# A fused attention and two-layer mixture kernel: gathering tokens into two buffers two groups ahead, an earlier table, and outputs block by block

## The chip, the cores and the metric

The kernel runs on one core of one Trainium2 chip. It uses five engines: TensorE (PE in the rows; PEld is its weight load), VectorE (DVE), ScalarE (ACT), GpSimd (POOL) and SyncE (SP), which only issues DMAs here. The metric is device time in microseconds of one execution; the median of the timed runs counts. One execution was taken with the hardware profiler.

## The reference

Three layers, all in float32:

```python
p_packed = sm_attn(p, k, v)              # 8 batches, 8 heads, 576 tokens, 32 packed rows, head size 64
out = sm_attn(q, p_packed, p_packed)
x = out.transpose(0, 2, 1, 3).reshape(4608, 512)
h = x @ w_in                             # 512 -> 2048
x = (h / (1 + exp(-h))) @ w_out          # 2048 -> 512
e = argmax(x @ w_gate, axis=1)           # one of 8 experts per token
for each expert:                         # 512 -> 1024 -> 512
    y = maximum(x[mask] @ w1[e], 0) @ w2[e]
    out[mask] = gate_w * sigmoid(x @ w_output_gate)[e] * y
```

`gate_w` is the softmax weight of the chosen expert. How many tokens an expert gets depends on the data.

## The kernel before

The first 800 us compute attention and the first mixture layer, batch by batch. Each block of 128 finished tokens is written to the DRAM table `xr` (a row is the 512 values and the gate weight), and its token numbers are scattered to the DRAM list `perm`, sorted by expert (`place`, L809). Matrix products are split: each float32 operand is a high and a low part, and three products are added. The expert weights were split earlier and lie in DRAM as `ws1` and `ws2`.

The change lies in the expert stage. Its unit is a **group**: 576 tokens of one expert, gathered through `perm`. Eight groups are laid out in the program (`NSTATIC`), more follow behind a branch that this data doesn't take. Group 0 is the largest expert's first 576 tokens, picked early. The others come from a table (`table`, `spread`) that is worked out once the last tokens are placed: expert and offset for each group, in the SBUF tile `tab`.

A group has 8 hidden slices of 128. For each slice n there is an **up projection** (`up`, L1002: 24 matmuls into the one PSUM tile `pu`), a handover (ScalarE takes the rectified high part, VectorE the low part, L1007 and L1008, into a ring of three), and a **down projection** (`down`, L1024 and L1027: 14 matmuls into five PSUM blocks of tokens). TensorE's order is up(n+1), gap, down(n), gap. The next up needs the handover of the one before, since `pu` has one buffer.

What else is to be done is hung into these **gaps** by number (`self.gaps`, 16 per group; group k owns gaps 16k to 16k+15). A step that is hung there is issued to its engines at that place of the program; each engine has its own queue and runs it in order.

- `fetch(g)`: SyncE reads expert and offset from `tab`, then orders the index table `xix` (from `perm`, L915 and L916) and the expert's gate row `og` (L934). GpSimd sets the unused indices (L914) and issues five indirect DMAs that gather the token rows to `xg` (L925).
- `trx(g, j)`: TensorE transposes block j of the gathered tokens (`px`, L966, one PSUM bank), ScalarE and VectorE copy and split it to `xt` (L971, L972); a gap later VectorE and ScalarE compute the output gate (`gate_dot`).
- `load_chunk`: SyncE orders a weight chunk of 2 MB for two slices (L950, L952) into a ring of five; it waits until the chunk that lay there has been used.
- `put_out(g, j)`, behind the last slice: ScalarE scales block j from PSUM to `y` (block 4 has two halves to add and goes over VectorE as well), and GpSimd scatters the rows to the output (L1046, an indirect DMA).

Gathered tokens, index tables and gate rows have one, three and one buffer. `plan` hangs the transposes of group k+1 into group k's gaps 5, 7, 9, 11 and 13 and the fetch of group k+2 into gap 15; in group 0 the transposes stand in gaps 12, 13, 14, 14 and 14. Behind the last group all engines load the number of groups from `tab` (L860) and branch.

Of the kernel before, what the change touches and what calls it, by code (L numbers as in the profile page):

```python
# [21 lines left out]
DM = 512  # L22
# [8 lines left out]
GB = 5  # L31
# [56 lines left out]
class Kernel:  # L88
# [762 lines left out]
    def experts(self):  # L851
        nc = self.nc
        g = self.group_l
        self.gaps = {0: [lambda: self.row_t(g, 4), self.load_chunk], 1: [lambda: self.row_logits(g, 4)], 2: [self.load_chunk],
                     3: [lambda: self.place(g)], 4: [self.table], 7: [self.spread, lambda: self.fetch(1)]}
        for i in (10, 13, 14, 15):
            self.gaps[i] = [self.load_chunk]
        self.plan(0, NSTATIC, 12, 1)
        self.groups(0, NSTATIC)
        t = nc.values_load(self.tab[0:1, 2, 0:1], min_val=0, max_val=NGRP)  # L860
        with self.tc.If(t > NSTATIC):
            self.more(NSTATIC, NSTATIC + 2)
            with self.tc.If(t > NSTATIC + 2):
                self.more(NSTATIC + 2, NGRP)

    def more(self, lo, hi):
        self.nload = 4 * lo
        self.fetch(lo)
        for _ in range(4):
            self.load_chunk()  # L870
        for j in range(GB):
            self.trx(lo, j)
        run(self.late)
        run(self.late)
        if lo + 1 < hi:
            self.fetch(lo + 1)
        self.plan(lo, hi)
        self.up(FG * lo)
        self.groups(lo, hi)

    def plan(self, lo, hi, first=5, every=2):
        for k in range(lo, hi - 1):
            at = [16 * k + (first + j * every if k == lo else 5 + 2 * j) for j in range(GB)]
            for j, n in enumerate(at):
                n = min(n, 16 * k + 14)
                self.gaps.setdefault(n, []).append(lambda k=k, j=j: self.trx(k + 1, j))
            if k + 2 < hi:
                self.gaps.setdefault(min(at[-1], 16 * k + 14) + 2, []).append(lambda k=k: self.fetch(k + 2))

# [9 lines left out]
    def groups(self, lo, hi):  # L899
        self.gap(2 * FG * lo)  # L900
        for n in range(FG * lo, FG * hi):
            if n + 1 < FG * hi:
                self.up(n + 1)
            self.gap(2 * n + 1)
            self.down(n)
            if n % 2 and n > 6 and self.nload < 4 * hi:
# [3 lines left out]
    def fetch_ix(self, g, off):  # L910
        nc = self.nc
        off = nc.values_load(off, engines=[ENG.SP], min_val=0, max_val=END)
        at = self.rt.tile([128, GB], I32, tag="xix", bufs=3, name="xix")
        nc.gpsimd.memset(at[64:128, 4:5], NTOK)  # L914
# [14 lines left out]
    def fetch(self, g):  # L929
        nc = self.nc  # L930
        self.expert(g)
        self.fetch_ix(g, self.tab[0:1, 0, g:g + 1])
        og = self.p2.tile([128, DM], F32, tag="og", name="og")
        nc.sync.dma_start(og, self.i["wog"][bass.ds(self.ex[g], 1), :].to_broadcast([128, DM]))  # L934
        x = self.rt.tile([128, GB, XW], F32, tag="xr", name="xg")
        self.x[g] = [x[:, j] for j in range(GB)], og
# [73 lines left out]

    def down(self, n):
        nc = self.nc
        g, ff = divmod(n, FG)
        w = self.chunk[n // 2][:, 2048:].rearrange("p (r k c) -> p r k c", r=2, k=2)[:, :, ff % 2, :]
        if ff % 2:
            self.chunk.pop(n // 2)
        hl = self.hl.pop(n)
        if ff == 0:
            self.acc = [(self.ps_acc if j < 4 else self.ps_a).tile([128, 512], F32, tag=f"acc{j}", name="py") for j in range(GB)]
        first, last = ff == 0, ff == FG - 1  # L1020
        for j in (4, 0, 1, 2, 3):
            if j == 4:
# [5 lines left out]
            if last:  # L1028
                self.put_out(g, j)
        if last:  # L1030
            self.at.pop(g)

# [52 lines left out]
```

## Time and profile before

| | us |
|---|---|
| median of 3 timed runs | 1304.09 (1303.91 to 1305.34) |
| profiled execution, its own time | 1306.18 |
| its span, first to last instruction | 1304.40 |
| TensorE matmul busy | 1213.3 |
| VectorE, ScalarE, GpSimd busy | 656.5, 472.6, 167.7 |

The expert stage begins at about 815 us. Busy times of TensorE are long where the clock is low, so idle time and the granted clock are read together. A row of the timeline may merge several instructions of a kind (x24); a bracket says how long the engine was idle before it and what its release is put down to. For TensorE the duration of a merged row reaches to the modelled end of its last matmul.

### The profile page before, as it was taken

How to read it: one execution, taken by the hardware profiler on the slowest of the kernel's cores; microseconds unless marked ns; L12 is line 12 of the kernel's file. 1: busy time of each engine (PE TensorE's matmuls, PEld its weight loads, DVE VectorE, ACT ScalarE, POOL GpSimd, SP SyncE). 2: the span in 40 equal slices, each digit the busy share in tenths (PEclk: the TensorE clock that was granted, in tenths of full speed). 3: DMA queues.
4: the chain of work that ended last, by engine and by line, in shares of the span. 5: the costliest groups of instructions: out<-in, count | busy, mean ns of one | idle time of the engine just before them, and what ended most of it. 6: DMA issues, size and time to landing. Idle time of an engine off the chain costs nothing. (4 is left out here: it accounts for less than half of the span.)

```text
span 1304.4 us, 22047 instructions
## 1 busy us (share of the span) xinstructions
PE 1213.3 (93%) x8758; PEld 1003.9 (77%) x8760; DVE 656.5 (50%) x1495; ACT 472.6 (36%) x978; POOL 167.7 (13%) x211
## 2 busy tenths in 40 slices
PE   7697998999998999999999999999989898998996
PEld 3575786877787787787777788898989898898995
DVE  6888658457657357658457545323313232232311
ACT  3333554454554354554454433112122121212221
POOL 0334101000101000101000401113020220302011
PEclk9898999999999999999999999999989999999998
DMA  8664468456767465867464711459454554637311
GB/s 304 214 182 168 166 231 267 169 206 229 269 217 253 164 233 200 260 230 252 172 217 161 213 48 34 124 209 322 175 206 158 214 203 178 215 133 273 132 37 39
DMA packets 118725, 250.26 MB, mean 192 GB/s; under 512 B 13363, under 2 KB 64374, under 8 KB 118358
## 3 DMA queue, kind: packets, MB, share of 16 engines
q1 hardware_dynamic: 111318, 228.66, 51.5%
q0 software_dynamic: 7296, 20.11, 4.2%
q8 instruction: 71, 1.16, 0.4%
q14 instruction: 40, 0.33, 0.1%
HBM read 160.17 MB, written 88.70 MB: 191 GB/s over the span
## 5 line engine op out<-in xcount | busy, mean ns | idle before, releaser
L741 PE MATMUL acc<-wo,ghi 128*128 128x512 f32 x1024 | 318.6, 392 | 0.0
L1002 PE MATMUL pu<-xt,w 128*128 128x256 f32 (+1 forms) x1536 | 224.6, 304 | 17.3 <-DVE xt L1008 17.3
L1002 PEld LDWEIGHTS pu<-xt,w 128*128 128x128 f32 x1536 | 218.0, 197 | 24.0 <-issue 19.4
L741 PEld LDWEIGHTS acc<-wo,ghi 128*128 128x128 f32 x1024 | 193.1, 189 | 38.3
L1008 DVE SCALAR_TENSOR_TENSOR xt<-pu,xt 128x512 fp32r<-128x512 f32 (+1 forms) x128 | 58.7, 458 | 325.3 <-ACT xt L1007 323.3
L741 PE MATMUL acc<-wo,glo 128*128 128x512 f32 x512 | 212.0, 414 | 0.0
L690 PE MATMUL ps_h<-a,m_hi 128*128 128x288 f32 x1024 | 211.2, 299 | 0.8 <-DVE a L656 0.8
L1027 PE MATMUL py<-w,xt 128*128 128x512 f32 x768 | 188.2, 393 | 0.2 <-issue 0.2
L690 PE MATMUL ps_h<-a,m_lo 128*128 128x288 f32 x512 | 161.4, 315 | 28.4 <-DVE g L700 19.6
L1007 ACT ACTIVATE xt<-pu 128x512 fp32r<-128x512 f32 (+1 forms) x128 | 52.5, 410 | 355.0 <-PE pu L1002 246.9
L1027 PEld LDWEIGHTS py<-w,xt 128*128 128x128 f32 x768 | 144.2, 188 | 34.3 <-issue 0.6
L690 PEld LDWEIGHTS ps_h<-a,m_hi 128*128 128x128 f32 x1024 | 167.3, 192 | 2.5 <-DVE a L656 1.0
L700 DVE SCALAR_TENSOR_TENSOR g<-g,ps_h 128x576 f32<-128x576 f32 x128 | 96.1, 750 | 133.2 <-ACT g L699 132.8
L699 ACT ACTIVATE g<-ps_h 128x576 f32<-128x576 f32 x128 | 83.3, 651 | 172.8 <-PE ps_h L690 160.2
L690 PEld LDWEIGHTS ps_h<-a,m_lo 128*128 128x128 f32 x512 | 97.8, 191 | 55.3 <-DVE g L700 28.9
L741 PEld LDWEIGHTS acc<-wo,glo 128*128 128x128 f32 x512 | 96.6, 189 | 45.6 <-issue 27.0
L809 POOL DMA_INDIRECT perm<-tok,dsti x36 | 39.0, 1083 | 653.9 <-DVE dsti L805 517.3
L710 DVE TENSOR_TENSOR glo<-g,ghi 128x512 fp32r<-128x512 f32 x128 | 91.5, 715 | 38.2 <-ACT ghi L705 33.7
L705 ACT CAST ghi<-g 128x512 fp32r<-128x512 f32 x128 | 79.4, 620 | 73.8 <-DVE g L700 72.3
L510 DVE TENSOR_TENSOR mid<-mid,shi 128x1024 fp32r<-128x1024 f32 x48 | 58.8, 1226 | 43.2 <-ACT shi L509 43.2
L925 POOL DMA_INDIRECT xg<-xr,xix x35 | 33.4, 955 | 239.6 <-DVE yl L1044 214.7
L561 PE MATMUL ps_m<-w_in,ppt 64*32 64x256 f32 x1008 | 44.8, 402 | 10.3 <-ACT e L577 6.1
(188 smaller groups left out, 1173.1 us busy)
## 6 DMA issues: line engine op xcount, KB each, us to landing
w<-ws SPq DMA_DIRECT2D x64, 1024.0 KB
ws<-shi SPq DMA_DIRECT2D x64, 512.0 KB
mid<-in_w SPq DMA_DIRECT2D x48, 512.0 KB
ws<-mid SPq DMA_DIRECT2D x48, 512.0 KB
att_v<-in_v SPq DMA_DIRECT2D x15, 640.0 KB
att_k<-in_k SPq DMA_DIRECT2D x15, 576.0 KB
xr<-xr SPq DMA_DIRECT2D x32, 256.5 KB
stg<-in_w_in SPq DMA_DIRECT2D x16, 512.0 KB
```

Source lines behind the costliest of these rows:

```text
L510: nc.vector.tensor_tensor(out=w.bitcast(F32R), in0=w, in1=hi.bitcast(F32), op=ALU.subtract)
L561: self.nc.tensor.matmul(ps[32 * c:32 * c + 32, r, :n], lhs(rows, c), rhs(rows, c), start=True, stop=True)
L690: nc.tensor.matmul(ps[:, hf, :288], lw[:, qd, fs], rx[:, qd, ts], start=(i == 0), stop=(i == 5))
L699: nc.scalar.activation(out=g2, in_=ps[:, :, :288], func=AF.Tanh, scale=0.5)
L700: nc.vector.scalar_tensor_tensor(out=g2, in0=g2, scalar=1.0, in1=ps[:, :, :288], op0=ALU.add, op1=ALU.mult)
L705: self.nc.scalar.copy(out=hi, in_=self.graw[:, :512])
L710: self.nc.vector.tensor_tensor(out=lo, in0=self.graw[:, :512], in1=self.ghi.bitcast(F32), op=ALU.subtract)
L741: self.nc.tensor.matmul(acc, l, r, start=(first and i == 0), stop=(last and i == 2))
L1002: nc.tensor.matmul(ps[:, hf, :m], w[:, k, r, fs], xt[:, l, k, ts], start=(i == 0), stop=(i == 11))
L1007: nc.scalar.activation(out=hi, in_=src, func=AF.Relu)
L1008: nc.vector.scalar_tensor_tensor(out=lo, in0=src, scalar=0.0, in1=hi.bitcast(F32), op0=ALU.max, op1=ALU.subtract)
L1027: nc.tensor.matmul(self.acc[j], hl[:, l + j * 128:l + j * 128 + 128], w[:, r], start=(first and i == 0), stop=(last and i == 2))
```

## The change

Gathered tokens have two buffers, one for odd and one for even groups, gate rows two and index tables four. The fetch of group k+2 stands in gap 3 of group k instead of gap 15; those of groups 1 and 2 in gaps 5 and 11 of group 0. In group 0 the last placement, the table and the spread stand in gaps 2, 3 and 5 (were 3, 4 and 7), a chunk load in 8 (was 10) and the five transposes in gaps 10 to 14. The number of groups is loaded six gaps before the end. In the last group the down projections of the last two slices are issued together, block by block, with each block's output behind it, in the order 0, 4, 1, 2, 3.

```diff
--- before.py
+++ after.py
@@ -851,17 +851,21 @@
     def experts(self):
         nc = self.nc
         g = self.group_l
-        self.gaps = {0: [lambda: self.row_t(g, 4), self.load_chunk], 1: [lambda: self.row_logits(g, 4)], 2: [self.load_chunk],
-                     3: [lambda: self.place(g)], 4: [self.table], 7: [self.spread, lambda: self.fetch(1)]}
-        for i in (10, 13, 14, 15):
+        self.gaps = {0: [lambda: self.row_t(g, 4), self.load_chunk], 1: [lambda: self.row_logits(g, 4)], 2: [lambda: self.place(g), self.load_chunk],
+                     3: [self.table], 5: [self.spread, lambda: self.fetch(1)], 11: [lambda: self.fetch(2)]}
+        for i in (8, 13, 14, 15):
             self.gaps[i] = [self.load_chunk]
-        self.plan(0, NSTATIC, 12, 1)
+        self.plan(0, NSTATIC, 10, 1)
+        self.gaps.setdefault(16 * NSTATIC - 6, []).append(self.total)
         self.groups(0, NSTATIC)
-        t = nc.values_load(self.tab[0:1, 2, 0:1], min_val=0, max_val=NGRP)
+        t = self.total_t
         with self.tc.If(t > NSTATIC):
             self.more(NSTATIC, NSTATIC + 2)
             with self.tc.If(t > NSTATIC + 2):
                 self.more(NSTATIC + 2, NGRP)
+
+    def total(self):
+        self.total_t = self.nc.values_load(self.tab[0:1, 2, 0:1], min_val=0, max_val=NGRP)
 
     def more(self, lo, hi):
         self.nload = 4 * lo
@@ -872,20 +876,19 @@
             self.trx(lo, j)
         run(self.late)
         run(self.late)
-        if lo + 1 < hi:
-            self.fetch(lo + 1)
+        for g in range(lo + 1, min(lo + 3, hi)):
+            self.fetch(g)
         self.plan(lo, hi)
         self.up(FG * lo)
         self.groups(lo, hi)
 
     def plan(self, lo, hi, first=5, every=2):
         for k in range(lo, hi - 1):
-            at = [16 * k + (first + j * every if k == lo else 5 + 2 * j) for j in range(GB)]
-            for j, n in enumerate(at):
-                n = min(n, 16 * k + 14)
+            for j in range(GB):
+                n = 16 * k + (first + j * every if k == lo else 5 + 2 * j)
                 self.gaps.setdefault(n, []).append(lambda k=k, j=j: self.trx(k + 1, j))
-            if k + 2 < hi:
-                self.gaps.setdefault(min(at[-1], 16 * k + 14) + 2, []).append(lambda k=k: self.fetch(k + 2))
+            if k > lo and k + 2 < hi:
+                self.gaps.setdefault(16 * k + 3, []).append(lambda k=k: self.fetch(k + 2))
 
     def rows_apart(self, name, put):
         self.tc.declare_no_dep(put, group=name, reason="every token has a row of its own")
@@ -902,7 +905,13 @@
             if n + 1 < FG * hi:
                 self.up(n + 1)
             self.gap(2 * n + 1)
-            self.down(n)
+            if n == FG * hi - 2:
+                continue
+            if n == FG * hi - 1:
+                m = n - 1
+                self.down(n, [(m, 4), (m, 0), (m, 1), (n, 0), (n, 4), (n, 1), (m, 2), (n, 2), (m, 3), (n, 3)])
+            else:
+                self.down(n)
             if n % 2 and n > 6 and self.nload < 4 * hi:
                 self.load_chunk()
             self.gap(2 * n + 2)
@@ -910,7 +919,7 @@
     def fetch_ix(self, g, off):
         nc = self.nc
         off = nc.values_load(off, engines=[ENG.SP], min_val=0, max_val=END)
-        at = self.rt.tile([128, GB], I32, tag="xix", bufs=3, name="xix")
+        at = self.rt.tile([128, GB], I32, tag="xix", bufs=4, name="xix")
         nc.gpsimd.memset(at[64:128, 4:5], NTOK)
         nc.sync.dma_start(at[:, 0:4], self.perm[bass.ds(off, 512), 0:1].rearrange("(j p) w -> p (j w)", p=128))
         nc.sync.dma_start(at[:64, 4:5], self.perm[bass.ds(off + 512, 64), 0:1])
@@ -930,9 +939,9 @@
         nc = self.nc
         self.expert(g)
         self.fetch_ix(g, self.tab[0:1, 0, g:g + 1])
-        og = self.p2.tile([128, DM], F32, tag="og", name="og")
+        og = self.p2.tile([128, DM], F32, tag="og", bufs=2, name="og")
         nc.sync.dma_start(og, self.i["wog"][bass.ds(self.ex[g], 1), :].to_broadcast([128, DM]))
-        x = self.rt.tile([128, GB, XW], F32, tag="xr", name="xg")
+        x = self.rt.tile([128, GB, XW], F32, tag="xr", name="xg") if g % 2 else self.p2.tile([128, GB, XW], F32, tag="xg", name="xg")
         self.x[g] = [x[:, j] for j in range(GB)], og
         self.fetch_x(g)
 
@@ -1008,17 +1017,17 @@
             nc.vector.scalar_tensor_tensor(out=lo, in0=src, scalar=0.0, in1=hi.bitcast(F32), op0=ALU.max, op1=ALU.subtract)
         self.hl[n] = hl
 
-    def down(self, n):
-        nc = self.nc
-        g, ff = divmod(n, FG)
-        w = self.chunk[n // 2][:, 2048:].rearrange("p (r k c) -> p r k c", r=2, k=2)[:, :, ff % 2, :]
-        if ff % 2:
-            self.chunk.pop(n // 2)
-        hl = self.hl.pop(n)
-        if ff == 0:
-            self.acc = [(self.ps_acc if j < 4 else self.ps_a).tile([128, 512], F32, tag=f"acc{j}", name="py") for j in range(GB)]
-        first, last = ff == 0, ff == FG - 1
-        for j in (4, 0, 1, 2, 3):
+    def down(self, n, parts=None):
+        nc = self.nc
+        if parts is None:
+            parts = [(n, j) for j in (4, 0, 1, 2, 3)]
+        for n, j in parts:
+            g, ff = divmod(n, FG)
+            w = self.chunk[n // 2][:, 2048:].rearrange("p (r k c) -> p r k c", r=2, k=2)[:, :, ff % 2, :]
+            hl = self.hl[n]
+            first, last = ff == 0, ff == FG - 1
+            if first and j == 4:
+                self.acc = [(self.ps_acc if i < 4 else self.ps_a).tile([128, 512], F32, tag=f"acc{i}", name="py") for i in range(GB)]
             if j == 4:
                 for i, r in enumerate((1, 0)):
                     nc.tensor.matmul(self.acc[4], hl[:, 512:2 * GN - 512], w[:, r], start=(first and i == 0), stop=(last and i == 1))
@@ -1027,8 +1036,6 @@
                     nc.tensor.matmul(self.acc[j], hl[:, l + j * 128:l + j * 128 + 128], w[:, r], start=(first and i == 0), stop=(last and i == 2))
             if last:
                 self.put_out(g, j)
-        if last:
-            self.at.pop(g)
 
     def put_out(self, g, j):
         nc, p2, acc = self.nc, self.p2, self.acc[j]
```

GpSimd's queue in the expert stage. `xix` is the index table, `xg` the gathered tokens, `out` the output; a row with x5 is a group's five gathers, `yl` and `y` its five scatters. Before, from the fetch of group 1 on:

```order
L914 MEMSET xix 64x1
L925 DMA xg<-xr,xix 128x513 x5
L1046 DMA out<-yl,xix 4608x512
L1046 DMA out<-y,xix 4608x512 x4
L914 MEMSET xix 64x1
L925 DMA xg<-xr,xix 128x513 x5
L914 MEMSET xix 64x1
L925 DMA xg<-xr,xix 128x513 x5
L1046 DMA out<-yl,xix 4608x512
L1046 DMA out<-y,xix 4608x512 x4
L914 MEMSET xix 64x1
L925 DMA xg<-xr,xix 128x513 x5
```

and now, from the same fetch:

```order
L923 MEMSET xix 64x1
L934 DMA xg<-xr,xix 128x513 x5
L923 MEMSET xix 64x1
L934 DMA xg<-xr,xix 128x513 x5
L1053 DMA out<-yl,xix 4608x512
L1053 DMA out<-y,xix 4608x512 x4
L923 MEMSET xix 64x1
L934 DMA xg<-xr,xix 128x513 x5
L1053 DMA out<-yl,xix 4608x512
L1053 DMA out<-y,xix 4608x512 x4
L923 MEMSET xix 64x1
L934 DMA xg<-xr,xix 128x513 x5
```

Before, from group 3 on, a group's five gathers stand directly ahead of the scatters of the group two before it. Now the two first fetches stand behind each other, and every later one follows the scatters.

TensorE's queue in the last group, from the last up projection's end. `w_11866` is the last weight chunk, `py_12030` to `py_12034` are blocks 0 to 4. Before (the first five rows are slice 62, the next five slice 63):

```order
L1024 MATMUL py_12034<-w_11866,xt0_8171 128x512 x2
L1027 MATMUL py_12030<-w_11866,xt0_8171 128x512 x3
L1027 MATMUL py_12031<-w_11866,xt0_8171 128x512 x3
L1027 MATMUL py_12032<-w_11866,xt0_8171 128x512 x3
L1027 MATMUL py_12033<-w_11866,xt0_8171 128x512 x3
L1024 MATMUL py_12034<-w_11866,xt0_8171 128x512 x2
L1027 MATMUL py_12030<-w_11866,xt0_8171 128x512 x3
L1027 MATMUL py_12031<-w_11866,xt0_8171 128x512 x3
L1027 MATMUL py_12032<-w_11866,xt0_8171 128x512 x3
L1027 MATMUL py_12033<-w_11866,xt0_8171 128x512 x3
```

and now:

```order
L1033 MATMUL py_12034<-w_11866,xt0_8171 128x512 x2
L1036 MATMUL py_12030<-w_11866,xt0_8171 128x512 x3
L1036 MATMUL py_12031<-w_11866,xt0_8171 128x512 x3
L1036 MATMUL py_12030<-w_11866,xt0_8171 128x512 x3
L1033 MATMUL py_12034<-w_11866,xt0_8171 128x512 x2
L1036 MATMUL py_12031<-w_11866,xt0_8171 128x512 x3
L1036 MATMUL py_12032<-w_11866,xt0_8171 128x512 x6
L1036 MATMUL py_12033<-w_11866,xt0_8171 128x512 x6
```

Block 0 is finished by the fourth row and block 4 by the fifth, where all blocks were finished in the last five rows.

TensorE's queue in group 0, at the transposes of group 1's tokens (`px`), with the up (`pu`) and down (`py`) projections between them. Before, from the first transposes on:

```order
L966 MATMUL px<-cst,xg 128x128 x4
L1002 MATMUL pu<-xt_8171,w 128x256 x12
L1002 MATMUL pu<-xt_8171,w 128x320 x12
L966 MATMUL px<-cst,xg 128x128 x4
L1024 MATMUL py<-w,xt_8171 128x512 x2
L1027 MATMUL py<-w,xt_8171 128x512 x12
L966 MATMUL px<-cst,xg 128x128 x12
L1002 MATMUL pu<-xt_8897,w 128x256 x12
```

and now, from behind the first transposes, which stand one up and one down projection earlier than before:

```order
L1011 MATMUL pu<-xt_8171,w 128x256 x12
L1011 MATMUL pu<-xt_8171,w 128x320 x12
L975 MATMUL px<-cst,xg 128x128 x4
L1033 MATMUL py<-w,xt_8171 128x512 x2
L1036 MATMUL py<-w,xt_8171 128x512 x12
L975 MATMUL px<-cst,xg 128x128 x4
L1011 MATMUL pu<-xt_8171,w 128x256 x12
L1011 MATMUL pu<-xt_8171,w 128x320 x12
L975 MATMUL px<-cst,xg 128x128 x4
L1033 MATMUL py<-w,xt_8171 128x512 x2
L1036 MATMUL py<-w,xt_8171 128x512 x12
L975 MATMUL px<-cst,xg 128x128 x4
```

The last three blocks stood in one piece, in one PSUM bank; now an up or a down projection stands between any two.

## Rows read from the trace of the kernel before

**Rows 1.** The page, part 1: busy us, share of the span, instructions.
```profile
PE 1213.3 (93%) x8758; PEld 1003.9 (77%) x8760; DVE 656.5 (50%) x1495; ACT 472.6 (36%) x978; POOL 167.7 (13%) x211
```

**Rows 2.** Waits from 800 us: who <- releaser: total us, times, longest.
```profile
PE pu L1002 <- DVE xt L1008: 17.3, 5, 3.6
...
PE px L966 <- DVE xt L972: 2.8, 2, 1.4
```

**Rows 3.** Timeline, group 2: start us, us, engine, line, operation [idle before <- releaser].
```profile
947.49 0.94 POOL L925 DMA_INDIRECT xg<-xr,xix  x1 [37.09 <-DVE yl L1044]
...
953.88 3.33 PE L1002 MATMUL pu<-xt,w 128*128 128x256 f32 x24
...
958.89 0.98 POOL L1046 DMA_INDIRECT out<-y,xix  x1 [0.30 <-issue]
...
962.07 0.60 ACT L1007 ACTIVATE xt<-pu 128x512 fp32r<-128x512 f32 x1 [9.61 <-PE py L1027]
...
964.05 6.03 PE L1002 MATMUL pu<-xt,w 128*128 128x256 f32 x24 [3.13 <-DVE xt L1008]
```

**Rows 4.** Timeline, group 7.
```profile
1241.21 2.97 PE L1027 MATMUL py<-w,xt 128*128 128x512 f32 x12
...
1244.78 0.91 POOL L1046 DMA_INDIRECT out<-yl,xix  x1 [47.05 <-DVE yl L1045]
...
1250.49 3.36 PE L1002 MATMUL pu<-xt,w 128*128 128x256 f32 x24
...
1253.95 0.60 ACT L1007 ACTIVATE xt<-pu 128x512 fp32r<-128x512 f32 x1 [4.89 <-PE pu L1002]
```

**Rows 5.** Timeline, group 1.
```profile
893.90 0.39 SPq L950 DMA_DIRECT2D w<-ws  x1
...
900.19 3.37 PE L1002 MATMUL pu<-xt,w 128*128 128x256 f32 x24
...
901.62 0.98 POOL L1046 DMA_INDIRECT out<-y,xix  x1 [0.30 <-issue]
...
904.29 0.99 POOL L925 DMA_INDIRECT xg<-xr,xix  x1 [1.56 <-PE pu L1002]
...
906.66 3.36 PE L1002 MATMUL pu<-xt,w 128*128 128x256 f32 x24
...
911.54 0.60 ACT L1007 ACTIVATE xt<-pu 128x512 fp32r<-128x512 f32 x1 [6.23 <-PE px L966]
```

**Rows 6.** Windows, group 2: engines' busy us (count), granted clock, DMA share, GB/s.
```profile
964.00:966.00 2.00, 1.95 (x9) 1.98 (x10) 0.00 (x0) 0.00 (x0) 0.00 (x0) 0.50 1.06 359
```

**Rows 7.** Timeline, group 6.
```profile
1201.73 4.94 PE L1002 MATMUL pu<-xt,w 128*128 128x256 f32 x24 [3.45 <-DVE xt L1008]
```

**Rows 8.** Timeline, the end of the program.
```profile
1285.92 0.63 PE L1024 MATMUL py<-w,xt 128*128 128x512 f32 x2
...
1289.11 0.62 PE L1024 MATMUL py<-w,xt 128*128 128x512 f32 x2
...
1290.44 2.73 ACT L1038 ACTIVATE y<-py,sc 128x512 f32<-128x512 f32 x4
...
1291.85 0.91 POOL L1046 DMA_INDIRECT out<-yl,xix  x1 [41.00 <-DVE yl L1045]
...
1296.94 0.98 POOL L1046 DMA_INDIRECT out<-y,xix  x1 [0.30 <-issue]
```

**Rows 9.** Line L925, the gathers: durations in ns, min/median/max.
```profile
L925 POOL DMA_INDIRECT xg<-xr,xix x35: 942/947/987, 865.6 to 1190.4; - x35
```

**Rows 10.** Timeline, group 0.
```profile
860.97 0.18 DVE L849 CAST tab<-ps_t 1x48 int32<-1x48 f32 x1
...
865.63 0.98 POOL L925 DMA_INDIRECT xg<-xr,xix  x1 [14.78 <-issue]
...
868.94 3.33 PE L1002 MATMUL pu<-xt,w 128*128 128x256 f32 x24
```

**Rows 11.** Line L860, the branch's value: durations in ns, first and last start.
```profile
L860 PEldq TENSOR_LOAD <-tab x1: 488/488/488, 1288.2 to 1288.2; - x1
```

## Prediction

> **What bounds the kernel now.** I read the page's busy shares first: TensorE matmul is at work 93% of the span [rows 1], so what can be gained is idle or slow time of TensorE, plus what lies behind its last matmul. The change is in the expert stage alone, so next came the waits from 800 us on [rows 2]. TensorE waits 17.3 us in five places before an up projection, and 2.8 us in two places before a transpose of gathered tokens. The rest of that stage runs without gaps.
>
> The timeline says what the five places are. Each is the fourth up projection of a group (of groups 2 to 6). For group 2 [rows 3]: the third one's matmuls end at 953.88 + 3.33 = 957.21 us, but ScalarE starts to read the result at 962.07, which is 4.86 us late. In group 7 [rows 4] the same step ends at 1250.49 + 3.36 = 1253.85 and ScalarE starts at 1253.95, as it should. What differs is GpSimd. In group 2 it issues ten indirect DMAs in a row, five gathers and five output scatters, from 947.49 to 958.89 + 0.98 = 959.87, and the late handover comes 2.2 us after the last of them. In group 7 it issues five scatters, from 1244.78, and they are over. In group 1 [rows 5] five scatters end at 901.62 + 0.98 = 902.60, there is a pause, five gathers start at 904.29: the up projection inside the pause (end 900.19 + 3.37 = 903.56) costs nothing, the one at the gathers' end (906.66 + 3.36 = 910.02) is taken up at 911.54, 1.52 us late, and TensorE lost nothing by it. So I read: while a row of indirect DMAs has been running for some time, TensorE's completions reach the others only about a microsecond or two after the row ends. The trace shows the pattern, not the reason.
>
> The cost of one such place is its wait and a slow projection behind it: the granted clock stands at 0.50, the lower level, after the idle stretch [rows 6], and the projection takes 4.94 us in group 6 [rows 7] and 6.03 in group 2 [rows 3], where 3.36 is usual. The sum comes from periods: the third up projection of group 1 starts at 900.19, of group 2 at 953.88, of group 7 at 1250.49 [rows 3 to 5]. The first period, which has no such place, is 53.69 us; the next five take 296.61, and 5 x 53.69 = 268.45. **The five places cost 28.2 us.**
>
> **The change, part by part.** *Gathers two groups ahead.* Let T be the end of a group's last down projection. Scatters start at T + 0.6 (T = 1241.21 + 2.97 = 1244.18, first scatter 1244.78) [rows 4]. Five of them take 6.1 us (1291.85 to 1297.92) [rows 8], so they end at T + 6.7. The gathers that before stood ahead of them in GpSimd's order now stand behind, and wait for their index table, which SyncE asks for right behind a 2 MB weight chunk that it issues at T. Group 1 of before has this very order: chunk at 893.90 = T, gathers at 904.29 = T + 10.4 [rows 5]. Ten in a row take 12.4 us [rows 3], so five gathers take 6.3 and end at T + 16.7. The up projections end at T + 9.7 and T + 16.1 (903.56 and 910.02) [rows 5]. The first of the two now falls between the rows of DMAs. The second is told late by what group 1 shows, 1.5 us, and group 1 shows also that this is just free: 911.54 plus the handover of 1.98 (962.07 to 964.05) [rows 3] is 913.52, and its next projection was due at 910.02 plus down projection and transposes, 3.5 us, the same time. So all 28.2 us go; I charge 0.2 us for each of the five for the edge: 28.2 - 1.0 = 27.2. What is late next is that second projection: each microsecond by which the gathers slip costs a microsecond there, and the slow clock if it is much; if they started 1.5 us sooner nothing would be lost.
>
> The rest of this part I cost at nothing. Behind the gathers, which now wait for their table, GpSimd has only the next group's scatters, some 37 us later. SyncE's table reads, index and gate-row loads move forward by twelve gaps, past three chunk loads; they take SyncE a few us and a chunk is used some four chunks after it is asked for. A table in a used buffer may have to wait for GpSimd's memset behind the scatters, at T + 6.7, and would land near T + 10 all the same. The second token buffer and second gate row only take waits away.
>
> By the Trainium skill's page "SBUF — State Buffer" (section "SBUF: two separate sides"), VectorE instructions that take the port pair it shares with GpSimd keep GpSimd from writing DMA descriptors, and the gathers now stand where VectorE does the group's hidden-layer work. By that rule they would stretch and the second projection would be told later, which is the first rival below. The trace does not bear it out: 35 gathers, some beside VectorE work, last 942 to 987 ns [rows 9].
>
> *First group.* Placement, table and spread move up by one or two gaps. VectorE copies the table out at 860.97, behind the spread's transposes, and the first gathers start at 865.63 [rows 10]. With the spread one unit of up and down (6.5 us, 900.19 to 906.66 [rows 5]) earlier, gathers start near 859.2 and end at 865.5; if the table's own chain on VectorE were late there, TensorE would wait for it, and the place of the placement one gap sooner is there to cover that. The transposes start two gaps earlier and have a gap each, where three stood in one gap with one PSUM bank and cost 2.8 us [rows 2]: that goes. But group 2's gathers follow. Their index table lies behind the first one, the gate row and a chunk in SyncE's order, and I take 8 to 9 us from the first gathers' start, by the 8 to 10 us that table and chunk took in group 1: they run from 868 to 874.3. The up projection that ended at 868.94 + 3.33 = 872.27 [rows 10] then falls into them and is told near 875, up to 3 us late, with 1.5 free; the transpose behind it needs the same bank. I charge 2.0. Bounds: -0.5 (the second row starts late enough) to 8 (both rows merge and it is told as late as in group 2).
>
> *Last group.* TensorE does the same 28 matmuls in another order, from 1285.92, fourteen in 3.19 us (to 1289.11) [rows 8], 0.23 each. Block 0 is done after eleven, at 1288.6; ScalarE takes 0.68 (2.73 for four) and the first scatter can go at 1289.6. Block 4 needs ScalarE and two VectorE steps and is ready near 1291.4; the other three follow at 1.27 each and the last starts at 1295.2, where it was 1296.94: 1.7 us off the end. The fourth block in the new order needs the last hidden slice at 1287.7, about when its handover ends, which may cost 0.3. Bounds: 1.7 to 0 (a late completion in the row of scatters holds block 3).
>
> *The branch's value* is loaded six gaps earlier. On TensorE's queue it took 488 ns at 1288.2 [rows 11], before the last 14 of its matmuls had started (1289.11 [rows 8]): the queue runs that far ahead, so it is hidden, 0; if the queue were not ahead it costs 0.5.
>
> **Sum.** 27.2 + 2.8 - 2.0 + 1.7 = 29.7 off, less about 1 for what moves in the boundaries that I can't place: 28.7. The profiled execution took 1306.18 (span 1304.40 and 1.78 around it); the median of the timed runs is 1304.09, 2.09 lower. Own time 1277.5, median **1275.4**.
>
> **Rivals.** *The late handover moves one projection on.* Index tables land later than T + 10.4 because scatters share the transfers with the chunk, and the projection that ends at T + 16.1 is told 3 to 4 us late: 2 us beyond the free 1.5, and about 1.5 us of slow clock, five times: +17, so 1292. For it: group 1 was at the very edge. Against: there scatters and chunk overlapped as well. By the Trainium skill's page "DMA: Bandwidth & Descriptors" (section "Issuing engines are not separate DMA queues") all transfers interleave on the same engines whoever starts them, so moving a gather saves no transfer time and it may collide with the chunk that follows at T + 13; that would be this case. The trace agrees only in part, since group 1's gathers did meet that chunk.
>
> *Scatters and gathers merge.* If the index table is there by T + 6.7, ten indirect DMAs run on end as before, only in the other order, until T + 13.0. The projection that ends at T + 9.7 is then told at T + 15.2, 5.5 us late, and costs 4.0 plus 1.6 to 2.7 of slow clock and some tenths, 6.4 instead of 5.6: five times +4, and the first group's two rows of gathers merge too, +6.4. With the 4.5 of the first and last group gone: +6, 1310, slower. It decides if the table lands within 6.7 us of T; in group 1 the gathers that wait for it started at T + 10.4. Against: the chunk is ahead of it.
>
> *The places stay for another reason* (the row of DMAs is a sign and not the cause; then the change doesn't do what it says): only the 4.5 less the 2.0 is left, 1301.6.
>
> **Chances.** Forecast 0.74 (own range 1270 to 1283), moved on 0.14, stays 0.06, merged 0.06. The measurement tells a change from none at 0.2%, 2.6 us. The case that stays lies at that edge and is split 0.03 and 0.03. Faster 0.74 + 0.14 + 0.03 = 0.91, same 0.03, slower 0.06. The range takes the forecast and most of the first rival: 1269 to 1290.
>
> **What would show it.** Right: no wait of TensorE over 0.5 us before an up projection after 880; the fourth projections of groups 2 to 6 at 3.4 us; gathers starting 9 to 12 us after a group's last down projection; eight-projection periods of 53 to 54 us; transposes of the first group without a wait; the last scatter under 3 us behind TensorE's last matmul. Wrong: ScalarE over 2 us late behind an up projection in every group (which one tells the rivals apart), GpSimd with ten indirect DMAs on end, or a granted clock of 0.5 after 900.

## The result and the profile after

The changed kernel takes 1271.34 us (median of 4 runs, 1270.72 to 1271.76) where the kernel before took 1304.00 beside it (4 runs, 1302.97 to 1305.34): 0.9749 of it, 95% interval 0.9732 to 0.9765. Forecast: 1275.4, range 1269 to 1290. Its profiled execution took 1271.73, its span is 1269.6 us.

The page, part 1 (busy us, share of the span, instructions), answers to [rows 1]: TensorE does the same work at 95% where it was 93%.

```profile
PE 1204.2 (95%) x8760; PEld 998.4 (79%) x8760; DVE 656.2 (52%) x1495; ACT 472.9 (37%) x978; POOL 168.9 (13%) x211
```

The waits of TensorE from 800 us on, whole (who <- releaser: total us, times, longest). Both lines of [rows 2], 17.3 before up projections and 2.8 before transposes, are gone:

```profile
PE ps_rt L254 <- ACT xr L752: 0.7, 1, 0.7
PE ps_rl L277 <- DVE mid L263: 0.5, 1, 0.5
```

Laid side by side from the starts of the up projections in the two timelines (third one of group 1: 900.19 and 895.75; third one of group 7: 1250.49 and 1217.77):

| stretch of the span | before | changed | difference | forecast |
|---|---|---|---|---|
| start to the first up projection | 814.89 | 813.45 | -1.4 | 0 |
| to the third of group 1 | 85.30 | 82.30 | -3.0 | -0.8 |
| six periods of eight, to the third of group 7 | 350.30 | 322.02 | -28.3 | -27.2 |
| to the end of the span | 53.91 | 51.83 | -2.1 | -1.7 |
| sum | 1304.4 | 1269.6 | -34.8 | -29.7, less 1.0 charged for boundaries |

The first line lies before anything that the change touches. The medians differ by 32.7 and not by 34.8, mainly because the profiled execution of before was 2.2 us over its median and that of the changed kernel 0.4.

One group's border in the changed kernel (timeline: start us, us, engine, line, operation, [idle before <- releaser]), to be held against [rows 3]:

```profile
943.77 0.93 POOL L1053 DMA_INDIRECT out<-yl,xix  x1 [34.80 <-DVE yl L1052]
...
948.92 0.99 POOL L1053 DMA_INDIRECT out<-y,xix  x1 [0.30 <-issue]
949.44 3.36 PE L1011 MATMUL pu<-xt,w 128*128 128x256 f32 x24
...
952.89 0.60 ACT L1016 ACTIVATE xt<-pu 128x512 fp32r<-128x512 f32 x1 [4.88 <-PE pu L1011]
...
955.50 0.99 POOL L934 DMA_INDIRECT xg<-xr,xix  x1 [5.48 <-DMA xix<-perm]
955.88 3.38 PE L1011 MATMUL pu<-xt,w 128*128 128x256 f32 x24
...
959.35 0.60 ACT L1016 ACTIVATE xt<-pu 128x512 fp32r<-128x512 f32 x1 [4.88 <-PE pu L1011]
...
960.57 0.95 POOL L934 DMA_INDIRECT xg<-xr,xix  x1 [0.30 <-issue]
...
962.79 3.36 PE L1011 MATMUL pu<-xt,w 128*128 128x256 f32 x24
```

The ten indirect DMAs are two rows of five now. The third up projection ends at 952.80, between the rows, and ScalarE takes it up at 952.89. The next ends at 959.26, inside the second row but only 3.8 us from its start, and is taken up at 959.35. No projection is slow any more: over the six periods TensorE is busy without a gap at full clock (windows, TensorE alone: the stretch, its length, busy us and instructions, granted clock, DMA share, GB/s).

```profile
895.75:1217.77 322.02, 322.02 (x1945) 1.00 0.57 201
```

The first group: the second row of gathers starts at 870.20, and the last three transposes follow without a wait.

```profile
857.78 0.98 POOL L934 DMA_INDIRECT xg<-xr,xix  x1 [8.49 <-issue]
...
870.20 0.95 POOL L934 DMA_INDIRECT xg<-xr,xix  x1 [6.29 <-DMA xix<-perm]
...
874.92 0.60 PE L975 MATMUL px<-cst,xg 128*128 128x128 f32 x4
...
878.55 0.60 PE L975 MATMUL px<-cst,xg 128*128 128x128 f32 x4
...
882.37 0.66 PE L975 MATMUL px<-cst,xg 128*128 128x128 f32 x4
```

The end, against [rows 8]: the first scatter goes out 2.9 us before TensorE's last matmul ends (1256.13 + 3.56 = 1259.69), the last one 2.8 us behind it, where it was 4.5 (1296.94 against 1289.56 + 2.88 = 1292.44; the first line below is of before).

```profile
1289.56 2.88 PE L1027 MATMUL py<-w,xt 128*128 128x512 f32 x12
...
1256.13 3.56 PE L1036 MATMUL py<-w,xt 128*128 128x512 f32 x15
1256.83 0.98 POOL L1053 DMA_INDIRECT out<-y,xix  x1 [38.62 <-ACT y L1045]
1258.67 0.91 POOL L1053 DMA_INDIRECT out<-yl,xix  x1 [0.86 <-DVE yl L1052]
...
1262.47 0.99 POOL L1053 DMA_INDIRECT out<-y,xix  x1 [0.30 <-issue]
```

### The profile page after: what moved, and what is told of

Its sections match the earlier page's. It is cut to its first block, busy times and chain, and to the rows that moved or that the text cites. A ratio compares the mean times of both kernels' runs of the same rounds, so it can differ in the third digit from the quotient of the medians.

```text
span 1269.6 us, 22035 instructions
## 1 busy us (share of the span) xinstructions
PE 1204.2 (95%) x8760; PEld 998.4 (79%) x8760; DVE 656.2 (52%) x1495; ACT 472.9 (37%) x978; POOL 168.9 (13%) x211
## 5 line engine op out<-in xcount | busy, mean ns | idle before, releaser
L1011 PE MATMUL pu<-xt,w 128*128 128x256 f32 (+1 forms) x1536 | 215.5, 296 | 0.0
L1011 PEld LDWEIGHTS pu<-xt,w 128*128 128x128 f32 x1536 | 209.6, 189 | 5.1
L509 ACT CAST shi<-mid 128x1024 fp32r<-128x1024 f32 x48 | 50.1, 1045 | 0.0
```

What stands on the lines that cost most here:

```text
L509: nc.scalar.copy(out=hi, in_=w)
L1011: nc.tensor.matmul(ps[:, hf, :m], w[:, k, r, fs], xt[:, l, k, ts], start=(i == 0), stop=(i == 11))
```

## The experiments

My theory (**row theory**): while a long row of indirect DMAs runs on GpSimd, TensorE's completions are held back until a microsecond or two behind its end. Rivals: it is the bytes on the way at once (**traffic**), or the single token buffer and its waits (**buffer**). The runs came to five chips, and that turned out to be the first finding: in some places nothing is held. A place here is the chip that a run happened to get, at that time. The ratio is taken from all runs of a row and can differ a little from that of the two medians.

| run | before beside it | its time | ratio, 95% interval |
|---|---|---|---|
| E1 ten in a row | 1272.19 | 1266.72 | 0.9947 (0.9929 to 0.9965) |
| E2 plain loads | 1272.19 | 1269.91 | 0.9976 (0.9960 to 0.9992) |
| E3 plain loads, tiny gathers | 1272.19 | 1269.07 | 0.9965 (0.9947 to 0.9983) |
| E4 placements in two rows | 1272.19 | 1266.64 | 0.9943 (0.9922 to 0.9965) |
| E5 changed kernel | 1272.09 | 1266.04 | 0.9951 (0.9933 to 0.9970) |
| E6 last group only | 1271.96 | 1270.70 | 0.9998 (0.9979 to 1.0016) |
| E7 first group only | 1271.96 | 1272.27 | 0.9997 (0.9983 to 1.0011) |
| E8 ten in a row | 1271.96 | 1265.86 | 0.9939 (0.9914 to 0.9963) |
| E9 split, tail order | 1271.96 | 1266.07 | 0.9953 (0.9936 to 0.9971) |
| E10 twenty in a row | 1307.86 | 1386.76 | 1.0586 (1.0549 to 1.0623) |
| E11 ten in a row | 1271.84 | 1267.06 | 0.9955 (0.9936 to 0.9974) |
| E12 both orders in one | 1305.16 | 1287.63 | 0.9862 (0.9833 to 0.9892) |

The kernel before takes 1303 to 1311 us in the places of the first result, of E10 and of E12, and 1269 to 1279 (medians about 1272) in those of the other ten. E1 to E4 came to one chip and E11, later, to the same; E5, E6 to E9, E10 and E12 to one each of four others. Which chip the first result is from is not recorded.

**E1, E8, E11: ten in a row.** The changed kernel with one number put back:

```diff
-                self.gaps.setdefault(16 * k + 3, []).append(lambda k=k: self.fetch(k + 2))
+                self.gaps.setdefault(16 * k + 15, []).append(lambda k=k: self.fetch(k + 2))
```

> The changed kernel with one thing put back: the fetch of group k+2 hangs in gap 15 of group k again (both token buffers, the four tables and the other two parts stay), so that GpSimd has the five gathers directly ahead of the five scatters. Row theory (a long row of indirect DMAs holds back TensorE's completions until a microsecond or two behind its end): the five late handovers come back, ScalarE about 4.8 us late behind the third up projection of groups 2 to 6, 28 us, so about 1299 us. Buffer theory (it was the single buffer and its waits that cost the time): no late handover, about 1271 us.

> The changed kernel with the fetch back in gap 15, a second time, in the hope of a place where completions are held. Where they are held (the kernel before at 1304 beside it), row theory: 1299, ScalarE about 4.8 us late in five places; buffer theory: 1271. Where they are not (before at 1272): 1266.5, no late completion, as the first time.

> The changed kernel with the fetch of group k+2 back in gap 15 (five gathers directly ahead of five scatters), a third time: twice the place had no hold. Where completions are held (before at 1304 to 1308 beside it): row theory, the five late handovers come back, ScalarE about 4.8 us late behind the third up projection of groups 2 to 6 and 28 us lost, so 1299 to 1303, 0.996 of before; buffer theory (the single token buffer cost the time), no late handover and 1271 to 1275, 0.975 of before. Where they are not held (before at 1272): 1266 again.

All three took about the time of the changed kernel in such a place (E5, 1266.04). The timeline of E1 shows why this is not an answer for the buffer theory: ten indirect DMAs run on end from 987.43 to 999.87, the up projection that ends in their midst at 994.70 is taken up at 994.79, and nothing was held here at all.

```profile
987.43 0.98 POOL L934 DMA_INDIRECT xg<-xr,xix  x1 [40.31 <-DMA xix<-perm]
...
991.33 3.37 PE L1011 MATMUL pu<-xt,w 128*128 128x256 f32 x24
...
994.79 0.60 ACT L1016 ACTIVATE xt<-pu 128x512 fp32r<-128x512 f32 x1 [1.70 <-PE pu L1011]
...
998.89 0.98 POOL L1053 DMA_INDIRECT out<-y,xix  x1 [0.30 <-issue]
```

So in this place the order of GpSimd's DMAs is worth nothing that the time shows, and the kernel before, at 1272.19, does not lose the 28 us.

**E2 and E3: the bytes without the row, and with a row that moves hardly any.** E3 has in addition, for each of the five, an indirect gather of 19 floats a row into a tile of its own.

```diff
+            if g > 1:
+                self.nc.sync.dma_start(x, self.xr[j * 128:j * 128 + 128, :])
+                continue
```

> The kernel before, in which the tokens of groups 2 to 7 are not gathered but loaded by five plain DMAs on SyncE, 128 rows each, the same bytes from other rows (so the output is that of other tokens). GpSimd then issues only the five scatters in a row. Row theory: the five late handovers go, ScalarE under 1.5 us late everywhere, 28 us less, about 1276 us. Traffic theory (the completions wait behind the bytes that gathers, scatters and the weight chunk move at once): nothing changes, ScalarE 4.8 us late in five places, about 1304 us.

> As the kernel with plain loads, and in addition five indirect gathers per group that move 19 floats a row into tiles that nobody reads (the same number of rows and instructions on GpSimd as before, 1/27 of their bytes). Row theory: ten indirect DMAs in a row again, the five late handovers are back, about 1304 us. Traffic theory: no difference to the kernel with plain loads, whatever that gave.

Both miss, and decide nothing: no completion was late in either, for the same reason.

**E5: the changed kernel again.**

> The changed kernel itself, unaltered, once more beside the kernel before. In the last four runs no completion of TensorE was late anywhere, and the kernel before took 1272 us there where it had taken 1304: the holding back was absent in them, whatever stood in GpSimd's row. Chip theory (the hold belongs to the chip or the place that a run gets): if this run gets one without it, before takes about 1272 and the changed kernel about 1266.5 us (only the first group's 3.0 and the last group's 2.1 us are left); if it gets one with it, before 1304 and changed 1271. Kernel theory (something in the changed kernel apart from the order of the DMAs makes it slow): changed 1271 whatever before takes.

As the chip theory expects: 1266.04. In a place that holds nothing back the change is still worth 0.5%, about 6 us. The trace also says where the changed kernel loses 5.3 us between the two places (1271.34 and 1266.04). Its first up projection starts 6.9 us earlier than in the first profile, at 806.60 instead of 813.45, and from there to the end of the span (1262.9) it takes 456.3 us against 456.2 (1269.6 - 813.45):

```profile
806.60 3.37 PE L1011 MATMUL pu<-xt,w 128*128 128x256 f32 x24
```

So with the rows apart the expert stage takes the same time in both kinds of place. What is left of the hold lies ahead of it: the three waits behind the placements' rows of five (1.35, 1.46 and 1.57 us in the first profile) are gone here.

**E6 and E7: the first and the last group's part alone,** each put into the kernel before (its list of gaps and `plan(0, NSTATIC, 10, 1)`; the new `down` and its order).

> The kernel before with nothing but the last group's part (down projections of the last two slices block by block, outputs in between); the number of groups is loaded where it was. Forecast's step: 1.7 us off; the two traces on record say 2.1. Where completions are held and where they are not, the same: before less about 2 us. Rival (the end is set by the last scatter's landing, whatever is issued first): no difference.

> The kernel before with nothing but the first group's part (placement, table, spread, chunk load and the five transposes moved as in the change; one token buffer and the fetches as before). The two waits of the transposes go, 2.8 us: before less about 3 us, with or without held completions. Rival (the earlier placement or table makes TensorE wait elsewhere, or the transposes wait for their tokens): no gain, or slower.

Neither shows a gain in time, so both expectations miss. In the traces the last group's part takes 1.5 us off the end (52.43 us from the third up projection of group 7 to the end in E6, 53.88 in E7), less than the intervals can tell. The first group's part does what it should, and loses it again. In E6, which has the old first group, the two waits of 1.4 us are there and the projection behind them is slow:

```profile
877.49 0.66 PE L972 MATMUL px<-cst,xg 128*128 128x128 f32 x4 [1.40 <-DVE xt L978]
879.55 0.66 PE L972 MATMUL px<-cst,xg 128*128 128x128 f32 x4 [1.40 <-DVE xt L978]
879.96 4.96 PE L1008 MATMUL pu<-xt,w 128*128 128x256 f32 x24
```

From the first up projection to the third of group 1 E6 takes 86.84 us and E7 82.26, 4.6 less. But in E7 the fetch of group 2 stands as late as before (gap 16, the first of group 1), and TensorE, now early, waits for its tokens:

```profile
896.74 0.99 POOL L925 DMA_INDIRECT xg<-xr,xix  x1 [5.63 <-PE py L1027]
...
903.87 1.12 PE L966 MATMUL px<-cst,xg 128*128 128x128 f32 x4 [3.98 <-DMA xg<-xr,xix]
```

With slow matmuls behind that wait the next period is 60.15 us instead of 53.67 (E6): 6.5 lost for 4.6 won. In the changed kernel the second fetch in gap 11 takes that wait away. So the first group's part is worth nothing without the early fetch; what the early fetch is worth without it no run shows.

**E4 and E9: the placements' scatters in two rows;** E9 also with the blocks of the last group in the order 0, 1, 4, 2, 3.

```diff
+                rows(range(2))
+                self.late.append(lambda: rows(range(2, n)))
```

> The changed kernel, in which the scatters of token numbers (four or five indirect DMAs of one word a row in one row, once for each batch but the last) are issued as two and, at the next step of the list of late work, the other two or three. In the changed kernel TensorE waits 1.35, 1.99, 1.46, 1.17 and 1.57 us (at 342, 408, 540, 604 and 735 us) behind these rows, 7.5 us in all. Row theory: a row of two or three is over before completions are held, the five waits go, about 1264 us. Rival (these waits come from the other work that VectorE does around the placement): the waits stay, 1271 us.

> The changed kernel with the placements' scatters in two rows and, in the last group, the blocks in the order 0, 1, 4, 2, 3, so that the second scatter does not wait for block 4's VectorE steps (0.86 us idle of GpSimd in the changed kernel). Where completions are held: 7.5 + 0.5 us under the changed kernel, about 1263.5. Where they are not: only the 0.5 us of the tail, about 1265.5 against before's 1272. Rival (block 1's scatter waits as long as block 4's did): nothing off the tail, 1266.

The edit did nothing: the five scatters still ran on end. Hung in later, they stand later in the program, but GpSimd has nothing in its queue between them and waits for nobody there. So this did not test the row theory. What the traces show all the same: the waits at 342, 540 and 735 us, behind rows of five, are gone in E4, E5 and E9, where nothing is held, and those at 408 and 604 us, behind rows of four, are there as before (1.96 and 1.14, where the first profile of the changed kernel had 1.99 and 1.17). So these two, which I had put down to the rows, have another cause. The new block order took 0.3 us off the end of the span (51.53 against 51.83 to 51.98 of the changed kernel's two profiles) and nothing that the time shows; no version is faster than the changed kernel by more than the intervals.

**E10: twenty in a row.** The kernel before, with ten gathers of three floats a row between a group's gathers and the scatters:

```diff
+        for j in range(10 if g > 1 else 0):
+            tiny = self.rt.tile([128, 3], F32, tag=f"tiny{j}", name="tiny")
+            self.nc.gpsimd.indirect_dma_start(out=tiny, out_offset=None, in_=self.xr[:n, :].rearrange("n (a b) -> (n a) b", b=3),
+                                              in_offset=bass.IndirectOffsetOnAxis(ap=at[:, j % 4:j % 4 + 1], axis=0))
```

> The kernel before, with ten more indirect DMAs between a group's five gathers (groups 2 to 7) and the scatters, each of three floats a row into tiles that nobody reads: twenty in a row on GpSimd, 25 us, with hardly more bytes. Where completions are held (before at 1304): row theory, the hold lasts until a microsecond or two behind the row's end, 12.7 us longer in each of five groups, so up to 63 us more, about 1360; traffic theory, 1304. Where they are not (before at 1272): if the row must only be longer there to start a hold, late handovers appear and it is slower by tens of us; if such a place has no hold at all, no handover is late and it takes 1272.

This run came to a place that holds: 1386.76 against 1307.86. One group border of its timeline:

```profile
957.42 0.94 POOL L925 DMA_INDIRECT xg<-xr,xix  x1 [32.97 <-DVE yl L1048]
...
963.89 3.37 PE L1006 MATMUL pu<-xt,w 128*128 128x256 f32 x24
...
981.30 0.98 POOL L1050 DMA_INDIRECT out<-y,xix  x1 [0.30 <-issue]
...
985.88 0.60 ACT L1011 ACTIVATE xt<-pu 128x512 fp32r<-128x512 f32 x1 [23.43 <-remote]
...
987.86 5.40 PE L1006 MATMUL pu<-xt,w 128*128 128x256 f32 x24 [17.33 <-DVE xt L1012]
```

The projection ends at 967.26 and is taken up at 985.88, 18.6 us later and 3.6 us behind the row's last DMA (982.28). In the midst of it next to nothing moves (window of six microseconds, DMA share 0.05; the columns are TensorE, its weight loads, VectorE, ScalarE, GpSimd, clock, share, GB/s):

```profile
970.00:976.00 6.00, 0.53 (x3) 0.09 (x1) 0.00 (x0) 0.00 (x0) 4.63 (x5) 0.93 0.05 1
```

and the five waits before an up projection sum to

```profile
PE pu L1006 <- DVE xt L1012: 81.1, 5, 17.7
```

where [rows 2] had 17.3: 63.8 more, as the row theory worked out (63). The trace has a sixth place, which the expectation did not count: in group 1 the gathers and the ten small ones make a row of fifteen.

```profile
905.55 0.98 POOL L925 DMA_INDIRECT xg<-xr,xix  x1 [2.14 <-DMA xix<-perm]
...
914.12 3.35 PE L1006 MATMUL pu<-xt,w 128*128 128x256 f32 x24
...
923.39 0.94 POOL L930 DMA_INDIRECT tiny<-xr,xix  x1 [0.30 <-issue]
...
927.23 0.60 ACT L1011 ACTIVATE xt<-pu 128x512 fp32r<-128x512 f32 x1 [13.76 <-remote]
```

The projection that ends at 917.47 is taken up 9.8 us late, 2.9 us behind the row's end (924.33), and the next one starts 15.8 us behind its start (at 929.93) where 6.9 is usual: 8.9 more. With that 72.7 of the 75.3 us between the two spans (1379.7 and 1304.4) are found; the rest is small and lies in slow projections (5.40 us above). The traffic theory, which had 1304, falls. Whether other long work on GpSimd than indirect DMAs would hold completions as well, no run tests.

**E12: both orders in one kernel.** Fetches in gap 3 for groups 1 to 3, in gap 15 for groups 4 and 5, so that one trace has its own control:

```diff
+                self.gaps.setdefault(16 * k + (3 if k < 4 else 15), []).append(lambda k=k: self.fetch(k + 2))
```

> The changed kernel with a control inside: the fetch of group k+2 hangs in gap 3 for groups 1 to 3 (as changed) and in gap 15 for groups 4 and 5 (five gathers directly ahead of five scatters); and of the placements' rows, one of five and one of four scatters (of batches 3 and 4, at about 533 and 604 us) are issued as two and the rest a step later, while those at 336, 408 and 730 us stay whole. Where completions are held (before at 1304 to 1308 beside it): row theory, periods of eight up projections of 53.7 us in groups 2 to 4 and 5 to 8 us longer twice around groups 5 and 6, and waits of TensorE of 1.3 to 2 us behind the whole placement rows, none behind the two split ones; buffer theory, no longer period; traffic theory, the split placements change nothing. About 1271 + 12 - 3 = 1280. Where they are not held (before at 1272): all periods 53.7, 1266.

A place that holds again. The periods of eight are 53.65, 53.68 and 53.58 us with the rows apart, then 59.37, 60.49 and 55.85: 14.6 us over 3 x 53.69, for two rows of ten (12 expected; the last figure has the second slow projection in it). Added to 1271.3 that is 1285.9, near the 1285.73 of the profiled execution; the 1280 expected also had 3 us taken off for the placements. At the first of them:

```profile
1099.26 0.99 POOL L942 DMA_INDIRECT xg<-xr,xix  x1 [42.50 <-DMA xix<-perm]
...
1103.37 3.35 PE L1019 MATMUL pu<-xt,w 128*128 128x256 f32 x24
...
1110.72 0.98 POOL L1061 DMA_INDIRECT out<-y,xix  x1 [0.30 <-issue]
...
1113.49 0.60 ACT L1024 ACTIVATE xt<-pu 128x512 fp32r<-128x512 f32 x1 [8.39 <-remote]
...
1115.43 5.07 PE L1019 MATMUL pu<-xt,w 128*128 128x256 f32 x24 [5.50 <-issue]
```

The projection ends at 1106.72 and is taken up at 1113.49, 6.8 us late and 1.8 us behind the row's end at 1111.70. With two token buffers the gathers start before the last down projection is over, so it is the second up projection of the group that is told late here, not the third. Two token buffers, the new tables and the new first and last group are the same in both halves of this kernel; only the gap of the fetch differs, and with it the order on GpSimd. The buffer theory falls. That the bytes of gathers and scatters also meet in the second half is the traffic theory, which E10 excludes. The placements stayed whole, as in E4, so that part of the expectation was not tested; the waits behind rows of five are back (1.15, 1.35 and 1.52 us).

## Why the prediction was right, and where it was not

The mechanism was right where it was read. The five late handovers were what a row of ten indirect DMAs costs in that place, and taking the rows apart gave the whole 28.2 us back (28.3 measured). E12 shows it by the order alone and E10 by the length of the row. What the forecast could not know from one trace: E5 shows the same program in a place without any hold, where the change is worth 6 us and not 33, and E1, E8 and E11 take about the same there with the rows put together again. So there was luck in the result: it was measured in a place like that of the trace from which the forecast was made, and the 1266.04 of E5 would have lain below the range. That the place decides is shown; that it is the chip is only suggested, by one chip that was met twice and did not hold either time.

*Edges, 1.0 charged, 0 paid.* The gathers did not start at T + 10.4 but 12.4 to 13.6 us behind a group's last down projection (955.50 - 943.13 = 12.4), outside the 9 to 12 that I had named. My rule that each microsecond of slip costs one there was wrong in sign: the up projection that I feared for now ends 2.4 to 3.8 us into the row instead of 5.7 [rows 5], and was told at once. A hold does not begin with the row; it had not begun at 3.8 us (above) and had at 5.7. In E10 a projection that ended 5.1 us into the row of fifteen (907.29 + 3.33 = 910.62) was taken up at 911.41, 0.8 us late and long before the row's end, so the beginning lies near there and is not sharp. This is also why the first rival did not cost anything: its later tables came, but later was safer. The forecast had not seen this; that the edge cost nothing is luck.

*First group, 2.0 charged for the second row of gathers, 0 paid.* It starts 12.4 us behind the first, not 8 to 9 (its table, ordered behind the first one's gate row and chunk, took 10.4 us from SyncE's order at 859.79), and the up projection that I placed inside it ended 1.2 us after its start. The 2.8 us of transposes are gone as forecast. The price 2.8 was right only for that execution: in E6 the projection behind the two waits is slow (4.96 us, where that of the first trace took 3.44), and the two runs differ by 4.6. And I had priced the three parts apart, though the first needs the second fetch (E7).

*Last group, 1.7 forecast, 2.1 measured.* From the third up projection of group 7 the last scatter starts after 44.70 us (1262.47 - 1217.77) instead of 46.45 (1296.94 - 1250.49): 1.75, the term as worked out. The other 0.3 lies behind it. *The branch's value:* forecast 0, and no wait of TensorE names it. But E6, which loads the number where it was, takes 7.68 us from the start of its last scatter (1261.22) to the end of its span, and the changed kernel 7.13 (first profile) and 7.29 (E5). So the early load may be worth some tenths at the very end; no run isolates it.

*What was held against it.* Gathers beside VectorE's work took 945 to 1187 ns, the median 949, against 947 before [rows 9]: that they would be stretched, as the Trainium skill's page "SBUF — State Buffer" (section "SBUF: two separate sides") has it for a time in which VectorE holds the port pair that the two share, is not seen, but for the one of 1187 ns at most. The other page that the prediction drew on, the Trainium skill's "DMA: Bandwidth & Descriptors" (section "Issuing engines are not separate DMA queues"), says that transfers interleave on the same engines whoever starts them. The gathers did come later (12.4 instead of 10.4 us behind T), but no run shows whether their tables met the chunk, and it cost nothing.

*The size.* In spans the gain was 6.1 us larger than the forecast's 28.7: 1.4 ahead of the stage, 2.2 in the first group, 1.1 in the six periods, 0.4 in the last group, and the 1.0 charged for boundaries. In medians it was 4.0 larger (32.7), since before's profiled execution lay 2 us above its median.

## What to carry to other kernels

Where a consumer takes a finished result up late, look at what GpSimd issues just then: a row of five indirect DMAs was harmless here where no completion fell into its second half (the placements' rows of five cost 1.35 to 1.57 us each in the first profile); ten on end cost 5.6 us (28.2 / 5) to 7.3 us (14.6 / 2) where completions are held. Break such rows with something that GpSimd really has to wait for (here the table's DMA); a later place in the program alone does not break them. And measure the kernel before again beside each run: the same two programs differed by 33 us in one place and by 6 in another (E5).

## What the runs showed of the hardware that was not expected

- In some places TensorE's completions are held back during a row of indirect DMAs, until 0.7 to 3.6 us behind its last one (E10; 1.2 and 1.8 in E12); in others not at all (0.09 us in E1, with the same row of ten). The cause of the difference stays open; nothing in the profile names the hold, its releasers read "remote" or "issue". The traces of the places that hold also have fewer records of semaphore updates (10,332 of before, 11,774 of E1), so it may be that the recording itself has a part in it; no run tests that.
- The number of DMAs in the row, or the time they take, counts, not the bytes: ten more gathers of 12 bytes a row (0.94 us each on GpSimd, as long as one of 2052 bytes) held the next handover back by 18.6 us instead of 4.9 [rows 3], at a DMA share of 0.05.
- A wait of TensorE costs more than its length: behind 17.33 us of idle the projection took 5.40 us (E10), behind 3.13 us 6.03 [rows 3], behind two waits of 1.4 us 4.96 (E6), where 3.36 is usual. It is not the same each time: behind the two waits of the first trace the projection took 3.44.
